# A spectral filter and a two-layer block on one core: the first batch's order of work, and the last chunk's stores

## The chip, the cores and the metric

The kernel runs on one core of a Trainium2 chip. The core has TensorE (PE, matrix products; its weight loads are shown apart as PEld), VectorE (DVE), ScalarE (ACT), GpSimd (POOL) and SyncE (SP, which only issues transfers). Transfers are issued from the queues of SP, ACT or POOL and carried out by 16 DMA engines. The metric is the device time of one execution in microseconds (us): the median of three runs before is 748.88 (748.31 to 749.69).

## The reference

```python
x: (8, 3008, 256)   filt_r, filt_i: (1505, 256)   w_in: (256, 2048)   w_out: (2048, 256)     # float32
X = np.fft.rfft(x, axis=1)
y = np.fft.irfft(X * (filt_r + 1j * filt_i)[None], n=3008, axis=1)    # a filter along the sequence
t = y.reshape(24064, 256)
h = t @ w_in
out = np.maximum(0.01 * h, h) @ w_out
```

## The kernel before

**The filter as matrix products.** 3008 = 94 x 32. A batch is transformed in four stages: s1 (94-point transform, one matmul for two of the 32 rows n2), s2 (twiddles and the 32-point transform, one matrix for each of 24 frequencies), the product with the filter, sa (inverse 32 points) and sb (inverse 94 points, which writes `yt`, the transposed activations of the current batch, 256 x 3008 in two halves dt). Between s1 and s2, and between sa and sb, the data must be turned. Batches 1 to 7 are turned through DRAM: staged in `st1` or `st2`, stored by SP to `dz1` or `dz2` (L264, L334), loaded back by SP (`t1_load` L271, `t2_load` L278). Every load of a batch's z1 needs all eight stores of its s1.

**The two-layer block.** Tokens go in 47 chunks of 512. `moe1` (L514) makes one column block ct of 16 for a chunk with two matmuls of 512; for every second ct ScalarE's leaky ReLU (L519) takes the pair from one of two wide accumulators (`ph`) to `gt`. The second layer of the first three chunks is `plain` (L639); from then on it is seven products of Strassen's scheme with 16 matmuls each (`products`, `product`, L578), whose sums VectorE makes (L551) and whose results VectorE combines into output rows (`rows`), stored by SP (`store`, L565).

**The loop's order** is a list sorted by plan time. SL = 8 units stand for one chunk; `PLANS` gives start and step of each stage of each batch in units, and a loop over a heap places the groups at least GAP = 0.6 units apart; z1 loads follow the last s1 group by AFTER[0] + LANDED = 2.96 units, and s2 a load by READ = 2.2. Each engine works through its own instructions in that order and waits on semaphores; POOL and SP, which have few, run ahead of TensorE.

**The first batch** has no earlier chunk to hide behind. Its steps are the string `FIRST`, executed one by one ahead of the loop: `xc` rounds early rows of x from fp32; `s1p` and `s1e` are s1's matmuls and their spread into big[0]; `t1` and `t2` are VectorE's transposes (big[0] to big[1], big[2] to big[0], four quarters each: quarters 0 and 1 are one half of the channels); `s2p` is s2's matmuls; the filter product is made by VectorE (`s2d`) or by ScalarE's copy (`s2a`, into one of six spare tiles) and POOL's product (`s2m`); `sap`, `sae` are sa and its copy, `sbp`, `sbe` sb and its copy to `yt`; `warm` is idle matmuls. A step's arguments are half, first row or frequency, count, part, accumulator (b0 to b4) or engine (A: ScalarE, D: VectorE). An `sb` group of half dt needs `t2` quarters 2 dt and 2 dt + 1.

Ahead of that string x comes in as follows: rows 0 to 5 by SP in fp32, rows 6 to 31 by three POOL transfers that round to fp16. POOL then issues the constants f2, the filter by halves of the channels, i1 and w_in, and, inside `FIRST`, the next batch's x in two halves and w_out. Ten of the sixteen last-stage groups are in `FIRST`; the other six are `late_sb`, put into the loop at the times `REST`. All of batch 1's s1 is in the loop.

**At the end** the last chunk has no later one beside it: its products run in the order m1, m7, m2, m6, m4, m5, m3, in turn on two accumulator banks, and its rows leave in 128 KB pieces. A tile of 128 tokens is one piece, or two where it crosses a boundary of 376 tokens.

Of the kernel before, what the change touches and what calls it, by code (L numbers as in the profile page):

```python
# [11 lines left out]
P = 128  # L12
# [63 lines left out]
def kernel(  # L76
# [134 lines left out]
    EARLY = 6  # L211
    x_early = big[1][:].bitcast(FP32)[:, : EARLY * D].rearrange("p (n d) -> p n d", n=EARLY)
    nc.sync.dma_start(small_sb[:], small_d.ap())
    nc.sync.dma_start(x_early[:R1], bass.AP(tensor=x.tensor, offset=x.offset, ap=[[N2 * D, R1], [D, EARLY], [1, D]]))
    for n0, nn in ((6, 10), (16, 10), (26, 6)):
        x_load(0, n0, nn)
# [8 lines left out]
    nc.gpsimd.dma_start(i1_sb[:], i1_d.ap())  # L225
    nc.gpsimd.dma_start(w_in_sb[:], moe_w_in.rearrange("(dt p) c -> p dt c", p=P))
# [27 lines left out]
    def s1_group(b, g, copy):  # L254
        def go():
            ps = bank("pf", 2, D)
            h = g // 2
            need(("x", b, h if b > 1 else 0), *[("st1", b, h - 4)] * (h > 3 and b > 1))
            nc.tensor.matmul(ps, fwd1[:N1], x_sb[:N1, ds(2 * g, 2), :], start=True, stop=True)  # L259
            issued.add(("s1", b, g))  # L260
            st = st1[h % 4] if b > 1 or h < 4 else st1_more[h % 4]
            copy(st[:, ds(2 * (g % 2), 2), :], ps)  # L262
            if g % 2:
                soon(AFTER[0], lambda: noted(("st1", b, h), lambda: nc.sync.dma_start(  # L264
                    dz1[b % 2][ds(4 * h, 4)].rearrange("n p d -> p n d"), st)))
        return go

# [95 lines left out]
    first_banks = single + wide  # L363
# [3 lines left out]
    def fill(key, b, n, w):  # L367
        held[key] = ps = first_banks[int(b[1:])][:, : n * w].rearrange("p (n w) -> p n w", n=n)
        return ps

    def keep_warm(n):
        for _ in range(n):
            nc.tensor.matmul(po_ps.rearrange("p a d -> p (a d)"), idle[:, 0:P], idle[:],  # L373
                             start=True, stop=True)

    def s1p(_, n0, n, b):
        ps = fill(("s1", n0), b, n, D)
        for j in range(0, n, 2):
            nc.tensor.matmul(ps[:, ds(j, 2), :], fwd1[:N1], x_sb[:N1, ds(n0 + j, 2), :],
                             start=True, stop=True)  # L380

    def s1e(_, n0, n, e):
        spread(big[0], n0, held.pop(("s1", n0)), engine[e])
# [6 lines left out]
    def s2p(hf, c, n, i, b):  # L390

        ps = fill(("s2", hf, c, i), b, n, DH)
        src = big[1][:].rearrange("p (n e r t) -> p n r e t", n=Q // 2, r=2, t=2)
        for j in range(n):
            v = src[:, (c + j) // 2, (c + j) % 2, ts(hf, DH // 2)]
            if i == 0:
                nc.tensor.matmul(ps[:, j, :].rearrange("p (e t) -> p e t", t=2), f2_sb[:, c + j, :], v,
                                 start=True, stop=True)
                continue
            for h in range(2):  # L400
                nc.tensor.matmul(ps[ts(h, 64), j, :].rearrange("p (e t) -> p e t", t=2),
                                 f2_sb[:, c + j, ts(1 - h, 64)], v, start=True, stop=True)
# [4 lines left out]
    def s2d(hf, c, n, i):  # L407
        times_filter(nc.vector, hf, c, n, i, held.pop(("s2", hf, c, i)))

    def s2a(hf, c, n, i):  # L410

        at_c = c if ("s2", hf, c, i) in held else c - 4
        held["xf", hf, c, i] = xf = spare.pop(0)
        key = ("s2", hf, at_c, i)
        act(xf[:], (held.pop(key) if c - at_c == n - 4 else held[key])[:, ds(c - at_c, 4), :])
# [35 lines left out]
    def late_sb(dt, h, copy):  # L451
        ps = bank("pf", 4, N1)
        sb_matmuls(ps, dt, h)
        quad_copy(h, dt, ps, copy)

    def load_x(half):
        x_load(1, half * N2 // 2, N2 // 2)
        issued.add(("x", 1, 0))

    def load_w_out():  # L460
        nc.gpsimd.dma_start(w_out_sb[:], moe_w_out.rearrange("(ct p) d -> p ct d", p=P))

    def round_x(n0, n, e):
# [3 lines left out]
        xc 0 4 A, xc 4 2 D, warm 18, s1p 0 0 4 b3, s1p 0 4 2 b0, warm 3, s1p 0 14 2 b1, s1e 0 4 2 D,  # L467
        s1e 0 0 4 A, s1p 0 10 4 b4, s1e 0 10 4 A, s1p 0 6 4 b3, s1e 0 14 2 D, warm 4, s1p 0 20 4 b4,
        s1e 0 6 4 D, s1p 0 16 4 b3, s1e 0 16 4 A, s1p 0 26 2 b2, s1p 0 24 2 b0, s1e 0 24 2 A, s1e 0 20 4 D,
        s1p 0 28 2 b1, s1p 0 30 2 b4, s1e 0 26 2 D, s1e 0 30 2 A, s1e 0 28 2 D, t1 0, t1 1, warm 14,  # L470
        s2p 0 0 4 0 b3, s2p 0 0 4 1 b2, warm 2, s2p 0 8 4 1 b0, s2a 0 0 4 0, s2a 0 0 4 1, t1 3,
        s2p 0 12 4 1 b4, t1 2, s2d 0 8 4 1, s2p 0 12 4 0 b1, s2p 0 16 8 0 b3, s2m 0 0 4 0, s2m 0 0 4 1,
        s2d 0 16 8 0, s2a 0 12 4 1, s2p 0 8 4 0 b2, s2p 1 16 8 0 b4, s2p 0 4 4 1 b0, s2a 0 12 4 0, s2d 0 8 4 0,
        s2a 1 16 8 0, s2p 0 4 4 0 b1, s2p 1 16 8 1 b3, s2d 0 4 4 0, s2a 1 20 8 0, sap 0 8 b2, s2d 0 4 4 1,
        s2a 1 16 8 1, s2a 1 20 8 1, s2m 0 12 4 0, s2p 0 16 8 1 b4, sap 0 0 b1, s2p 1 0 8 1 b3, s2m 0 12 4 1,
        sap 0 12 b0, s2m 1 20 8 0, sae 0 8 A, s2d 0 16 8 1, sae 0 0 A, s2p 1 8 8 1 b4, sap 0 4 b2, s2d 1 0 8 1,
        sap 0 16 b1, sae 0 12 A, s2p 1 8 8 0 b3, sap 0 20 b0, s2d 1 8 8 1, s2m 1 20 8 1, sae 0 4 A,
        s2d 1 8 8 0, s2p 1 0 8 0 b4, sae 0 16 A, sap 1 20 b2, s2d 1 0 8 0, sap 1 12 b1, sae 0 20 A, sap 1 8 b0,
        x 0, s2m 1 16 8 0, sae 1 20 A, s2m 1 16 8 1, x 1, w_out, sae 1 12 A, sae 1 8 A, sap 1 16 b3,
        sae 1 16 A, sap 1 4 b2, t2 1, sae 1 4 A, sap 1 0 b4, t2 0, sae 1 0 A, warm 4, sbp 0 1 b1, sbp 0 4 b0,  # L480
        sbp 0 0 b3, sbp 0 3 b2, t2 3, sbe 0 1 A, sbe 0 4 A, sbe 0 0 A, sbp 0 2 b4, sbp 0 7 b1, sbp 0 6 b0,
        t2 2, sbe 0 2 A, sbe 0 7 A, sbp 0 5 b3, sbp 1 0 b4, sbp 1 1 b1, sbe 0 6 A, sbe 0 5 A, sbe 1 1 A,
        sbe 0 3 D, sbe 1 0 D
    """
    steps = dict(s1p=s1p, s1e=s1e, t1=t1, s2p=s2p, s2d=s2d, s2a=s2a, s2m=s2m, sap=sap, sae=sae, t2=t2,
                 sbp=sbp, sbe=sbe, x=load_x, w_out=load_w_out, xc=round_x, warm=keep_warm)
# [15 lines left out]
    gts, osts, phs = {}, {}, {}  # L502
# [39 lines left out]

    def quarter(ci, i, j):
        return gts[ci][:, ts(j, NCH), ts(i, TH)]
# [12 lines left out]
    def store(ci, tj, of, queue=nc.sync):  # L557

        t, end = ci * CH + tj * P, ci * CH + (tj + 1) * P
        lo = 0  # L560
        while t < end:
            e = min(end, (t // QT + 1) * QT)
            b, h = divmod(t // QT, N2 // 4)
            row = b * N + (t % QT) // 4 * N2 + 4 * h
            queue.dma_start(  # L565
                bass.AP(tensor=out.tensor, offset=out.offset + row * D,
                        ap=[[N2 * D, (e - t) // 4], [D, 4], [1, D]]), of[lo : lo + e - t])
            lo, t = lo + e - t, e

    def product(ci, a, w, after, last_sum=None):  # L570

        po = out_banks[done["products"] % 2][:, 0]
        done["products"] += 1

        def one(t, c):
            if last_sum is not None:
                need(("sum", ci, last_sum))
            nc.tensor.matmul(po[:, t], a()[:, c, ts(t, P)], w[:, c, :],  # L578
                             start=(c == 0), stop=(c == NCH - 1))
            if t == 1 and c == NCH - 1:  # L580
                after(po)
        return [lambda t=t, c=c: one(t, c) for t in range(2) for c in range(NCH)]
# [7 lines left out]
    def stores(ci, i, of=range(2)):  # L590
        for j in of:
            store(ci, 2 * i + j, rows(ci, i)[:, j, 0:2, :].rearrange("p k d -> p (k d)"),
                  nc.scalar if ci == NCHUNK - 1 and i == j else nc.sync)
# [13 lines left out]
    def products(ci):  # L607
# [9 lines left out]
        def m2():  # L617
            return product(ci, a12, b21, lambda po: add(rows(ci, 0)[:, :, 0], po, t1, AL.add))
# [3 lines left out]

        if ci == NCHUNK - 1:
            items = last_product(ci - 1) + m1() + m7() + m2()
        elif ci > W0:
# [4 lines left out]
        items += product(ci, lambda: sum_places(ci)[2], wt[1], lambda po: add(part[1], twice(po), part[0], AL.add), 2)  # L630
        items += product(ci, a22, wt[3], lambda po: add(rows(ci, 1)[:, :, 0], po, u3, AL.add))
        items += product(ci, lambda: sum_places(ci)[0], wt[0], after5, 0)
        return items + last_product(ci) if ci == NCHUNK - 1 else items
# [15 lines left out]
    for g in range(10, 16):  # L649
        at(REST[g - 10], lambda g=g: late_sb(1, g - 8, (act, dve)[g % 2]))  # L650

    def plan(b, s1, s1_step, s2, s2_step, lag, sb, sb_step, xl, x_step):
        for g in range(16):
            groups.append((s1 + s1_step * g, 1, b, g, s1_group(b, g, dve if b == 1 and g % 4 < 3 else act)))
            if g % 2 and b + 1 < B:
# [28 lines left out]
    last, when, place, loads = -1, {}, {}, {}  # L684
# [32 lines left out]
    for ci in range(NCHUNK + 1):  # L717
        if ci < NCHUNK:
            for ct in range(NCT):
# [43 lines left out]
```

## Time and profile before

| | us |
|---|---|
| median of three runs | 748.88 |
| the profiled execution, time | 748.2 |
| its span, first to last instruction | 746.4 |
| first matmul of the loop (L514) | 34.56 |
| first s2 matmul of batch 1 (L308) | 59.64 |
| last matmul's end, by the chain of waits | 741.38 |

| engine | busy, us | share of the span |
|---|---|---|
| TensorE matmuls | 737.3 | 99% |
| weight loads | 528.6 | 71% |
| ScalarE | 559.1 | 75% |
| VectorE | 502.2 | 67% |
| GpSimd | 168.4 | 23% |

Matmuls are pipelined, so the duration of one (0.38 us for 512 columns) is longer than the distance to the next. The chain of waits goes back from the last instruction, at each step to what released it; its steps show what one instruction costs in a row of its kind. In the views of the queues q0 is POOL's queue and q1 SP's; a share over 100% is time of several packets at once on an engine.

### The profile page before, as it was taken

Reading aid. Unit: us, or ns where it says so; the run is one execution under the profiler, and the core shown is the slowest. Engines: PE = TensorE matmul, PEld = TensorE weight load, DVE = VectorE, ACT = ScalarE, POOL = GpSimd, SP = SyncE. Lnnn points to the kernel's source line nnn. Section 1 sums busy time; section 2 is a strip of 40 time slices with the busy share of each in tenths; the row PEclk is TensorE's granted clock in tenths of the full one; section 3 lists DMA queues with packets and bytes.
Section 4 is the critical chain, followed back from the end, with each engine's and each line's share of the span. In section 5 each row is a group of like instructions: output and inputs, shape, how many; then the busy total and the mean of one; then the engine's idle time right before and its main releaser. Section 6 shows DMA issues by size and latency. Waiting matters only on the chain.

```text
span 746.4 us, 19411 instructions
## 1 busy us (share of the span) xinstructions
PE 737.3 (99%) x8017; PEld 528.6 (71%) x8017; DVE 502.2 (67%) x684; ACT 559.1 (75%) x755; POOL 168.4 (23%) x171
## 2 busy tenths in 40 slices
PE   8999999999999999999999999999999999999997
PEld 3556667676687777877778777777777777777776
DVE  5987637776686766766767667766676676465565
ACT  4776797888878787877777777787777777777662
POOL 5603412332222222121332322121212210000000
PEclk9999999999999999999999999999999999999999
DMA  9997797978875666755675656544454333111012
GB/s 205 228 225 197 189 229 214 216 187 214 215 178 147 161 196 161 173 138 156 199 179 144 158 164 171 158 133 111 144 165 118 100 108 107 52 54 54 29 49 66
DMA packets 119560, 113.64 MB, mean 152 GB/s; under 512 B 16352, under 2 KB 92768, under 8 KB 119280
## 3 DMA queue, kind: packets, MB, share of 16 engines
q1 hardware_dynamic: 104128, 94.66, 42.6%
q0 software_dynamic: 15056, 17.49, 16.0%
q8 instruction: 62, 1.02, 0.6%
q10 hardware_dynamic: 288, 0.26, 0.1%
q14 instruction: 26, 0.21, 0.1%
HBM read 57.51 MB, written 50.33 MB: 144 GB/s over the span
## 4 chain that ended last, share of the span: by engine, by line
PE 95%; DVE 2%; DMA 1%; ACT 1%; issue 0%; SPq 0%; DVEq 0%; ACTq 0%
PE ph L514 43%; PE po_ps L578 18%; PE pf L578 18%; PE pf L259 3%; PE pf L351 3%; PE pf L308 2%; PE pf L330 2%; PE pf L639 1%; PE po_ps L639 1%; DMA big<-in_x_dram 1%; PE po_ps L373 1%; DMA dz<-big 0%; DVE big L551 0%; ACT yt L341 0%; PE pf L442 0%
## 5 line engine op out<-in xcount | busy, mean ns | idle before, releaser
L519 ACT ACTIVATE gt_c<-ph 128x1024 f16<-128x1024 f32 x376 | 385.3, 1025 | 133.5 <-PE ph L514 122.7
L514 PE MATMUL ph<-yt,w_in_sb 128*128 128x512 f16 (+7 forms) x1728 | 447.3, 351 | 0.2 <-ACT yt L341 0.2
L578 PEld LDWEIGHTS <-gt_c 128*128 128x128 f16 x2800 | 202.2, 98 | 91.1
L323 POOL TENSOR_TENSOR y_b_g<-p_b_g,p_b_g 128x512 f16<-128x512 f32 x84 | 118.7, 1414 | 413.1 <-DMA p_b_g<-p_b_g 222.9
L578 PEld LDWEIGHTS <-big 128*128 128x128 f16 x2128 | 151.3, 98 | 61.6 <-issue 0.2
L514 PEld LDWEIGHTS <-w_in_sb 128*128 128x128 f16 x1728 | 137.5, 98 | 19.7 <-DVE yt L341 0.4
L317 DVE TENSOR_TENSOR p_b_g<-pf,fb_sb 128x512 f32<-128x512 f32 x78 | 53.6, 688 | 31.6 <-PE pf L308 13.3
L578 PE MATMUL po_ps<-wt_sb,gt_c 128*128 128x128 f16 x704 | 70.0, 219 | 0.1
L578 PE MATMUL pf<-wt_sb,gt_c 128*128 128x128 f16 x688 | 68.4, 219 | 0.0
L578 PE MATMUL pf<-w_out_sb,gt_c 128*128 128x128 f16 x720 | 67.9, 219 | 0.0
L578 PE MATMUL po_ps<-wt_sb,big 128*128 128x128 f16 x720 | 67.4, 219 | 0.0
L578 PE MATMUL pf<-wt_sb,big 128*128 128x128 f16 x704 | 67.2, 219 | 0.0
L262 ACT CAST big<-pf 128x512 f16<-128x512 f32 x98 | 57.1, 588 | 11.9 <-PE pf L259 10.5
L578 PE MATMUL po_ps<-w_out_sb,gt_c 128*128 128x128 f16 x688 | 66.0, 219 | 0.0
L341 ACT CAST yt<-pf 128x376 f16<-128x376 f32 x120 | 56.3, 473 | 11.0 <-PE pf L351 8.1
L551 DVE TENSOR_TENSOR gt_c<-gt_c 128x2048 f16<-128x2048 f16 x43 | 57.2, 1331 | 1.0
L320 DVE TENSOR_TENSOR p_b_g<-pf,fa_sb 128x512 f32<-128x512 f32 x84 | 57.2, 680 | 0.2
L551 DVE TENSOR_TENSOR big<-gt_c 128x2048 f16<-128x2048 f16 (+1 forms) x46 | 55.8, 1214 | 0.1
L551 DVE TENSOR_TENSOR big<-gt_c,big 128x2048 f16<-128x2048 f16 (+1 forms) x45 | 55.8, 1240 | 0.0
L551 DVE TENSOR_TENSOR big<-big,gt_c 128x2048 f16<-128x2048 f16 (+1 forms) x45 | 55.4, 1232 | 0.1
L332 ACT CAST big<-pf 128x512 f16<-128x512 f32 x84 | 49.0, 584 | 4.9 <-PE pf L330 3.0
L259 PE MATMUL pf<-x_sb,small_sb 94*128 94x512 f16 x109 | 41.6, 381 | 0.0
(91 smaller groups left out, 621.9 us busy)
## 6 DMA issues: line engine op xcount, KB each, us to landing
dz<-big SPq DMA_DIRECT2D x98, 256.0 KB
p_b_g<-p_b_g SPq DMA_DIRECT2D x156, 128.0 KB
out_dram<-ost_c_h SPq DMA_DIRECT2D x118, 128.0 KB
big<-dz SPq DMA_DIRECT2D x42, 256.0 KB
big<-dz SPq DMA_DIRECT2D x56, 192.0 KB
x_sb<-in_x_dram POOLq DMA_DIRECT2D x40, 192.0 KB, 4.4
x_sb<-in_x_dram POOLq DMA_DIRECT2D x2, 768.0 KB, 9.3
w_in_sb<-in_moe_w_in_dram POOLq DMA_DIRECT2D x1, 1024.0 KB, 13.8
```

What stands on the lines that cost most here:

```text
L259: nc.tensor.matmul(ps, fwd1[:N1], x_sb[:N1, ds(2 * g, 2), :], start=True, stop=True)
L262: copy(st[:, ds(2 * (g % 2), 2), :], ps)
L317: nc.vector.tensor_tensor(p2[:], ps, fb, AL.mult)
L320: nc.vector.tensor_tensor(p1[:], ps, fa, AL.mult)
L323: ("y", b, g), lambda: nc.gpsimd.tensor_tensor(y1[:], p1[:], p3[:], AL.add)))
L332: nc.scalar.copy(st2[h % 4][:, ds(2 * (g % 2), 2), :], ps)
L341: copy(yv, ps.rearrange("p c a -> p a c"))
L351: nc.tensor.matmul(ps[:, j, :], z2[h % 4][:K4, j, ts(dt, P)], i1_sb[:K4, 4 * h + j, :], start=True, stop=True)
L514: nc.tensor.matmul(ph[:, j, ds(t - ci * CH, e - t)], w_in_sb[:, dt, ts(ct, P)], yt[:, dt, ds(t % N, e - t)], start=(dt == 0), stop=(dt == ...
L519: nc.scalar.activation(gts[ci][:, ds(2 * g, 2), :], ph, AF.Lrelu)
L551: nc.vector.tensor_tensor(*(v[:, ds(c0, n)] for v in (o, i0, i1)), op)
L578: nc.tensor.matmul(po[:, t], a()[:, c, ts(t, P)], w[:, c, :], start=(c == 0), stop=(c == NCH - 1))
```

## The change

- **x of batch 0.** Rows 0 to 11 come early in fp32, by two SP transfers of six rows; the rest by POOL in pieces of 8, 8 and 4. The small constants move from SP's queue to ScalarE's. Six `xc` steps of two rows round the early rows.
- **s1 by halves of the channels.** `s1p` and `s1e` take "a" (all 256), "l" or "r" (128 each). Rows 20 to 31 go by halves.
- **A sixth accumulator** for `FIRST`: the output bank po_ps is b3, the wide ones become b4 and b5. `warm` names its bank.
- **Moved into `FIRST`:** the six late last-stage groups; eight s1 groups of batch 1 (`bp`, `be`, with their stores to dz1 placed in the loop); the first four column blocks of chunk 0 (`la` and `lb` are the two halves of the contraction, `le` the leaky ReLU).
- **POOL's loads** become steps: x0 and i1 after the first transposes, then w_in in two halves (w0, w1), x1 and w_out after POOL's ten products.
- **A new order** of all steps.
- **The last chunk:** order m1, m7, m2, m6, m5, m4, m3, each from m6 on in banks of its own; the two halves of its tokens change places (`token_half`); the left half of the rows that m2 completes is stored at once; m4 and m3 are combined and stored tile by tile, by SP and ScalarE, the last ones as half rows (64 KB).
- **The planner** starts from the columns and groups already done (`begun`, `ahead`).

```diff
-    EARLY = 6
+    EARLY = 12
...
-    nc.sync.dma_start(small_sb[:], small_d.ap())
-    nc.sync.dma_start(x_early[:R1], bass.AP(tensor=x.tensor, offset=x.offset, ap=[[N2 * D, R1], [D, EARLY], [1, D]]))
-    for n0, nn in ((6, 10), (16, 10), (26, 6)):
+    for n0 in range(0, EARLY, 6):
+        nc.sync.dma_start(x_early[:R1, ds(n0, 6)], bass.AP(tensor=x.tensor, offset=x.offset + n0 * D,
+                                                           ap=[[N2 * D, R1], [D, 6], [1, D]]))
+    nc.scalar.dma_start(small_sb[:], small_d.ap())
+    for n0, nn in ((12, 8), (20, 8), (28, 4)):
         x_load(0, n0, nn)
...
-    nc.gpsimd.dma_start(i1_sb[:], i1_d.ap())
-    nc.gpsimd.dma_start(w_in_sb[:], moe_w_in.rearrange("(dt p) c -> p dt c", p=P))
...
-    first_banks = single + wide
+    first_banks = single + [po_ps.rearrange("p a d -> p (a d)")] + wide
...
+    halves = {"a": ds(0, D), "l": ds(0, DH), "r": ds(DH, DH)}
+    def s1p(d, n0, n, b):
+        at, w = halves[d], halves[d].size
+        ps = fill(("s1", d, n0), b, n, w)
+        m = CH // w
+        for j in range(0, n, m):
+            nc.tensor.matmul(ps[:, ds(j, m), :], fwd1[:N1], x_sb[:N1, ds(n0 + j, m), at], start=True, stop=True)
...
+    def load(what):
+        if what == "i1":
+            nc.gpsimd.dma_start(i1_sb[:], i1_d.ap())
+        elif what == "w_out":
+            nc.gpsimd.dma_start(w_out_sb[:], moe_w_out.rearrange("(ct p) d -> p ct d", p=P))
+        elif what[0] == "x":
+            x_load(1, int(what[1]) * N2 // 2, N2 // 2)
+            issued.add(("x", 1, 0))
+        else:
+            part = ts(int(what[1]), DFF // 2)
+            nc.gpsimd.dma_start(w_in_sb[:, :, part], moe_w_in.rearrange("(dt p) c -> p dt c", p=P)[:, :, part])
+    def next_s1p(g, b):
+        ps = fill(("next", g), b, 2, D)
+        nc.tensor.matmul(ps, fwd1[:N1], x_sb[:N1, ds(2 * g, 2), :], start=True, stop=True)
+    def next_s1e(g, e):
+        engine[e](st1_of(1, g // 2)[:, ds(2 * (g % 2), 2), :], held.pop(("next", g)))
+    def first_l1(k, dt):
...
+        if dt == 0:
+            first_ph[k] = bank("ph", 2, CH)
+        for j in range(2):
+            nc.tensor.matmul(first_ph[k][:, j, :], w_in_sb[:, dt, ts(2 * k + j, P)], yt[:, dt, :CH],
+                             start=(dt == 0), stop=(dt == NDT - 1))
+    def lrelu(k):
+        nc.scalar.activation(gts[0][:, ds(2 * k, 2), :], first_ph.pop(k), AF.Lrelu)
...
     FIRST = """
+        warm 13 b4, xc 0 2 A, xc 4 2 D, xc 2 2 D, s1p a 0 2 b0, warm 3 b2, xc 6 2 D, xc 8 2 A, s1e a 0 2 A,
...
+        s1p r 28 4 b0, s1p r 24 4 b2, s1e l 28 4 A, warm 13 b3, s1e a 10 2 D, s1e r 28 4 A, t1 0, s1e r 24 4 A,
+        t1 1, load x0, t1 3, s2p 0 4 4 0 b0, load i1, s2p 0 0 4 0 b1, s2p 0 12 4 1 b2, s2p 0 4 4 1 b3, t1 2,
...
+        sae 0 16 A, s2m 1 4 4 1, s2d 1 0 4 1, sap 1 16 b5, sae 1 8 A, s2p 1 20 4 1 b2, t2 1, sae 1 16 A, bp 4 b0,
+        s2m 1 12 4 1, bp 2 b1, be 4 A, bp 0 b3, sap 1 0 b5, s2d 1 20 4 1, be 2 A, bp 5 b0, s2m 1 12 4 0,
+        sap 1 4 b4, be 0 A, sae 1 0 D, sap 1 20 b1, be 5 A, t2 0, bp 7 b2, load w0, bp 1 b3, sae 1 4 A,
+        sap 1 12 b0, load w1, sae 1 20 A, sae 1 12 D, sbp 0 1 b5, be 1 A, load x1, sbp 0 0 b1, t2 2, sbe 0 1 A,
+        sbp 0 7 b4, load w_out, sbp 0 5 b3, sbe 0 0 A, sbp 0 6 b5, sbe 0 5 A, sbp 0 4 b1, t2 3, sbe 0 7 A,
...
+        be 7 D, sbp 1 0 b3, sbe 1 2 A, sbp 1 4 b1, la 0, sbe 1 0 D, sbe 1 7 A, sbe 1 4 A, bp 6 b0, la 1, be 6 A,
+        lb 0, lb 1, le 1, le 0
     """
...
+    def token_half(ci, i):
+        return 1 - i if ci == NCHUNK - 1 else i
...
+        if ci == NCHUNK - 1:
+            free = [w[:, :CH].rearrange("p (a t d) -> p a t d", a=2, t=2)[:, 0] for w in wide + single]
+            return last_product(ci - 1) + m1() + m7() + m2(ci) + m6(free[0]) + last_three(ci, free[1:])
...
+        def m4_tile(t, po):
+            add(high[:, t, 0], po, u3[:, t], AL.add)
+            parts = list(pieces(ci, t, high[:, t, 0:2, :].rearrange("p k d -> p (k d)")))
+            parts.sort(key=lambda v: -v[1].shape[0])
+            soon(0.02, lambda: (nc.sync, nc.scalar)[t].dma_start(*parts[0]))
+            for v in parts[1:]:
+                soon(0.6, lambda v=v: nc.sync.dma_start(*v))
+        def m3_tile(t, po):
+            add(low[:, t, 1], po, high[:, t, 2], AL.add)
+            soon(0.02, lambda: store(ci, 2 + t, low[:, t, 1], P, P, queue=(nc.sync, nc.scalar)[t]))
...
-    for g in range(10, 16):
-        at(REST[g - 10], lambda g=g: late_sb(1, g - 8, (act, dve)[g % 2]))
+    ahead, begun = FIRST.count(" bp "), 2 * FIRST.count(" lb ")
+    for h in range(ahead // 2):
+        at(begun / 2 + 0.7 + 0.8 * h, lambda h=h: st1_store(1, h))
...
-    last, when, place, loads = -1, {}, {}, {}
+    last, when, place, loads = begun / 2 - GAP, {(1, 1, g): 0 for g in range(ahead)}, {}, {}
...
-            for ct in range(NCT):
+            for ct in range(0 if ci else begun, NCT):
```

## The prediction, on record before any run of the change

> **What bounds the kernel now.** I read the page first: busy shares and slices, then the chain of waits.
>
> ```profile
> span 746.4 us, 19411 instructions
> ...
> PE 737.3 (99%) x8017; PEld 528.6 (71%) x8017; DVE 502.2 (67%) x684; ACT 559.1 (75%) x755; POOL 168.4 (23%) x171
> ...
> PE 95%; DVE 2%; DMA 1%; ACT 1%; issue 0%; SPq 0%; DVEq 0%; ACTq 0%
> ```
>
> The reader is to see that TensorE is the bound. From the first L514 matmul (34.56) to the last one (741.38) are 706.8 us. The steps of the chain price the work: 0.43 us for two 512-column matmuls (0.217 each), 0.44 for four of L639 (0.11), 0.39 for seven of L578 (0.056). Counted out over 47 chunks and seven batches this gives about 706, so the loop has no holes. Its time falls only by work that leaves TensorE's list, and any new wait in it is paid in full. Outside it lie 34.56 us ahead and 5.0 behind. The profiled execution took 748.2 us; the median of the runs is 748.88, 0.7 above it. Differences are added to 748.88.
>
> The chain of waits over the first 50 us:
>
> ```profile
> 27.75 1.21 DVE prod L405
> 28.96 2.29 DVE big L434 x2
> 31.30 0.46 PE pf L442 x8
> 31.78 2.74 ACT yt L341 x7
> 34.56 0.38 PE ph L514
> ```
>
> VectorE's filter products and transposes come last, then ScalarE's copies of the last stage. The timeline adds who feeds them:
>
> ```profile
> 16.80 0.71 POOL L226 DMA_DIRECT2D w_in_sb<-in_moe_w_in_dram  x1 [0.54 <-DMA fa_sb<-in_filt_i_dram]
> 18.23 4.52 POOL L405 TENSOR_TENSOR prod<-spare,fa_sb 128x512 f16<-128x512 f32 x4 [0.71 <-ACT spare L415]
> 23.05 2.29 POOL L405 TENSOR_TENSOR prod<-spare,fa_sb 128x512 f16<-128x512 f32 x2 [0.30 <-ACT spare L415]
> ...
> 28.12 0.57 POOL L196 DMA_DIRECT2D x_sb<-in_x_dram  x1
> 28.69 1.18 POOL L461 DMA_DIRECT2D w_out_sb<-in_moe_w_out_dram  x1
> ```
>
> At 23.05 POOL waits on "spare", but that copy ended by 21.6: the filter's second half landed then. w_in, second x and w_out were issued between POOL's products, so the DMA engines never ran dry: they are busy in every slice from 2 to 50 us. Two views of the queues over one microsecond each show who had them (packets, MB, share of the engines), the first from 39 to 40 us, the second from 42 to 43:
>
> ```profile
> q0 software_dynamic: 391, 0.20, 146.6%
> ```
> ```profile
> q1 hardware_dynamic: 442, 0.22, 78.1%
> ```
>
> Until w_out is through (about 41.6) POOL's queue has all of it; SP's first dz store, issued at 37.44, moves nothing before 41. Then SP's 2.9 MB (eight stores and the new f2) flow until 50 to 53, and the loads that need them follow:
>
> ```profile
> 37.44 1.55 SPq L264 DMA_DIRECT2D dz<-big  x2
> ...
> 40.41 10.68 SPq L264 DMA_DIRECT2D dz<-big  x6
> 51.18 4.26 SPq L565 DMA_DIRECT2D out_dram<-ost_c_t  x2
> 55.66 1.86 SPq L271 DMA_DIRECT2D big<-dz  x4
> ```
>
> **Moved work.** Out of the loop go eight s1 groups (8 x 0.217 = 1.73), four columns ct of chunk 0 (eight matmuls, 1.73) and six late sb (0.38 each, 2.28): 5.74 us. Break-even is therefore a loop that starts at 34.56 + 5.74 = 40.30.
>
> **New prologue.** The small constants (0.37 us of issue, 0.13 MB) leave SP's queue for ScalarE's, so the first six rows land some 0.8 us sooner (before: 6.88); rows 6 to 11 share with POOL's casts and land between 7.5 and 9.5. As fp32 they take 0.59 MB at 0.36 MB/us instead of 0.295 MB at 0.21: 0.2 us more, which the earlier start pays. The last rows stay at 12.3, where POOL's L204 saw them; their matmul (0.38) and spread (0.61) end at 13.3, and half-d lets the first two transposes start then, since they need the left half alone. VectorE's own list before them (six x casts and spreads, if rows 6 to 11 are late) makes it 14.2 at worst; before, 14.66. Four transposes at 1.16, then seven products of the first half at 0.62 (1.87 for three), end near 22.9; the filter's second half still lands at 23.2. So VectorE gains nothing: from 23.3 six products (3.7; fourteen in all where there were sixteen, POOL has ten for eight), t2 1.18, a product 0.62, two sae at 0.66, three more t2 (3.5) end at 33.8 against 33.59. ScalarE then carries more: copies of 512 come 0.48 apart (two in 1.07), sbe 0.36 apart (two in 0.85). From sae 1 16 (27.65) eight such copies 3.9, thirteen sbe 4.7, be 3 and be 6 1.0: 37.2; lb 1 is ready at 37.9; two Lrelu 2.0. They come as "le 1, le 0", while the loop's first matmul writes the bank of le 0, so TensorE waits for both: start 39.9 to 40.7. I take 40.3, the two last steps being the nearest rows: **0 us**, between -1.3 (transposes' gain passed on whole) and +1.5 (three missed copies).
>
> **Early clock.** The first idle matmuls are 0.43 apart, after 4.47 us 0.20. The new order leaves TensorE idle some 2 us near 8. The Trainium skill ("TensorE: Matmul & The Clock Gate", Part 1: The HAM clock gate) says an idle window of about 3.4 us halves the clock again. By it sixteen s1 matmuls could cost 3.5 us more; by the row, which holds a pause of 1.2 us without loss, nothing.
>
> **Loads.** x0 and i1 follow the filters (end 21.5): 0.79 MB at the 0.21 MB/us of casts, 0.77 MB at 0.36, done at 27.4. But w0, w1, x1 and w_out stand behind ten POOL products: from 17.9, ten at 1.13 end at 29.2. With an issue of 0.7 and 1 us to start, the engines idle about 3.5 us. The four need 2.5 + 2.5 + 3.75 + 5.4: w0 lands about 35 (la 0 needs 36.5, hidden), x1 about 41 (s1 g8 needs 41.6, no room), w_out's bytes end at 45, not 41.6, landing 46 to 48 where L639 wants it at 47.2. What is late next is batch 1's z1. POOL, which runs ahead, also puts four x loads of batch 2 behind w_out by 37 us; before, two. Two more are 0.39 MB, 1.9 us; dz had the larger share after 42 (78% against 38% for POOL's queue), so half of it counts. SP, which also runs ahead, issues the stores of the groups moved in and the new f2 from 32 us, behind w0 or among the four; the sum of the bytes stays. The backlog ends at 50 + 3.5 + 0.95 + 0.2 (more fp32 in x) = 54.65. Add 1.6 to land (last output bytes at 744.8, end 746.4) and 3.2 for z1, which is the median of a 128 KB x load: 59.45. Meanwhile the planner, with s1 finished at 7.36 units and not 9.68, puts the first s2 of batch 1 at 12.95 units, not 14.9: 40.3 + 12 columns 5.2 + eight s1 1.73 = 47.2, plus 4.95/8 of a chunk (32 x 0.217 + 64 x 0.11 = 14.0) and one s1: 56.1. TensorE would stand 3.35 us in all, at x1, w_out or this s2, with all chunk 1 behind it; on SP the output stores wait behind z1's loads. Bounds: 0 if dz writes pass everything (the last one issued at 48, 3.8 us as from 742.61 to 746.4, 3.2 for z1: 55.0, in time), 5.3 with a gap of 3.8, both x loads ahead, and z1 taking the 3.9 of 55.66 to 59.53 (61.4). I take **+3.35**, since the row at 39 us shows SP waiting behind POOL's loads, not passing them.
>
> The Trainium skill ("DMA: Bandwidth & Descriptors", Anatomy of one DMA) prices a POOL transfer at 2 us plus bytes over 436 GB/s. An estimate by that: the four loads (5.8 MB of source) end at 44.5, dz and f2 are out near 51, s2 is on time, and the sum is 747.6. The trace moved dz at 0.33 to 0.35 MB/us and landed w_out 15.9 us after its issue, where the page's price alone gives 6.8; so the measurement decides.
>
> **The end.**
>
> ```profile
> 741.23 1.47 ACTq L565 DMA_DIRECT2D out_dram<-ost_c_h  x2
> 741.40 0.42 DVE L603 TENSOR_TENSOR ost_c_h<-pf,ost_c_h 128x256 f32<-128x256 f32 x1 [0.20 <-PE pf L578]
> ...
> 742.61 0.91 SPq L565 DMA_DIRECT2D out_dram<-ost_c_h  x1
> ```
>
> Own banks remove the 0.2 us before 737.58 (m6 waited for L621). The last add shrinks from 0.42 to about 0.28 (512 columns 0.69, 256 0.42). One store of 64 KB on ACT replaces SP's two pieces: issue over at 742.2, not 743.5. The 512-byte runs may eat some. **-1.3**, between -1.7 and -0.5. Six adds by tile lie under the matmuls (0.45 a tile).
>
> **Sum.** 0 + 3.35 - 1.3 = +2.05: 750.9 us.
>
> **Rivals.** *The loads come in time.* For it: the before kernel had 1 us of slack at 55.66, and dz writes got the larger share after 42. Against: the idle gap. Stall 0 to 1: 748.88 - 1.3 + 0.5 = 748.1. *The prologue pays and loads come in time.* For it: transposes can start 1.25 sooner and ScalarE idles 1.9 us between 17 and 27.7. Against: the filter at 23.05. 748.88 - 1.3 - 1.3 = 746.3; it decides if the loop starts before 39.2 and s2 of batch 1 runs by 55. *The change does not do what it says*, the tail's small rows taking as long as before: 0.8 more on any of these.
>
> **Numbers.** Late loads 0.55 (749.4 to 752.9), in time 0.23, prologue pays 0.22. A measurement tells about 0.2% (1.5 us) from no change, so slower is 0.55, same 0.23 and faster 0.22. The range goes from 746.2, the paying prologue, to 752.9, the full price of late loads.
>
> **What would show it.** Right: TensorE idle for 2 us or more between 41 and 62 on x_sb, w_out_sb or big<-dz (L259, L639, L308); DMA near empty about 28 to 31; first loop matmul at 40.3 after le 0; last add to end 0.9 shorter. Wrong: no such wait, first s2 of batch 1 by 57; or a loop start before 39 or after 42.

## The result, and the profile after

The changed kernel takes **756.34 us** (754.87 to 762.95, 6 runs) beside 748.95 (748.07 to 749.69, 6 runs) of the kernel before on the same chip: ratio **1.0115 [1.0091, 1.0139]**. It is slower, as forecast, but by 7.4 us and not by 2; 756.3 lies above the range (746.2 to 752.9). The profiled execution took 755.19 us with a span of 753.4, 7.0 above the span before, and that difference is what follows.

The page of the changed kernel (busy shares and the share of each engine in the chain that ended last):

```profile
span 753.4 us, 19393 instructions
...
PE 737.0 (98%) x8001; PEld 528.5 (70%) x8001; DVE 499.4 (66%) x687; ACT 563.1 (75%) x767; POOL 168.4 (22%) x174
...
PE 90%; DMA 5%; POOL 2%; DVE 2%; issue 1%; ACT 0%; SPq 0%; POOLq 0%
```

TensorE's busy time is the same (737.0 after 737.3); most of the 7 us is time in which it stands. Transfers have gone from 1% of the chain to 5%. The whole list of what TensorE waited for after 40 us is below (line, releaser, us in all, times, longest); before, it held one entry of 0.2 us.

```profile
PE po_ps L722 <- DMA w_out_sb<-in_moe_w_out_dram: 3.1, 1, 3.1
PE ph L555 <- ACT gt_c L495: 2.1, 1, 2.1
PE pf L358 <- DMA big<-dz: 0.8, 1, 0.8
PE pf L315 <- ACT big L262: 0.6, 2, 0.4
PE pf L259 <- DMA x_sb<-in_x_dram: 0.3, 1, 0.3
PE po_ps L630 <- DVE big L680: 0.3, 1, 0.3
PE pf L358 <- DVE p_b_g L327: 0.2, 1, 0.2
```

The chain of waits from 30 to 63 us (start, us, what), and POOL's timeline that leads into it:

```profile
30.64 1.44 POOL w_in_sb L472 x2
32.07 11.55 DMA x_sb<-in_x_dram
...
43.66 0.59 PE pf L259
...
52.17 0.96 SPq L272
...
53.23 6.41 DMA dz<-big
...
59.83 2.97 DMA big<-dz
...
62.84 0.38 PE pf L315 x2
```
```profile
19.40 11.23 POOL L418 TENSOR_TENSOR prod<-spare,fa_sb 128x512 f16<-128x512 f32 x10 [1.23 <-ACT spare L426]
30.59 1.49 POOL L472 DMA_DIRECT2D w_in_sb<-in_moe_w_in_dram  x2
32.07 0.56 POOL L196 DMA_DIRECT2D x_sb<-in_x_dram  x1
32.60 1.20 POOL L466 DMA_DIRECT2D w_out_sb<-in_moe_w_out_dram  x1
```

The reader is to see one sequence: ten products in a row on POOL, then the four loads that the loop's start needs, then TensorE waiting at x1 (43.66) and at w_out (54.13). Batch 1's first s2 starts at 62.84 (before 59.64), as soon as its z1 has landed. Ahead of the loads the DMA engines stand empty. Four windows of the changed kernel (stretch; busy time and count of PE, PEld, DVE, ACT, POOL; granted clock; DMA share; GB/s):

```profile
12.00:14.00 2.00, 2.00 (x6) 0.73 (x5) 1.24 (x3) 1.40 (x3) 1.59 (x3) 0.50 1.44 275
...
28.00:30.00 2.00, 2.00 (x17) 0.95 (x16) 2.00 (x3) 2.00 (x6) 2.00 (x3) 1.00 0.05 21
30.00:32.00 2.00, 1.84 (x11) 0.62 (x10) 2.00 (x4) 2.00 (x6) 2.00 (x3) 1.00 0.04 8
...
44.00:46.00 2.00, 2.00 (x6) 0.73 (x5) 1.06 (x2) 0.86 (x1) 0.00 (x0) 0.52 1.06 345
```

A share of 0.05 and 0.04 is an empty engine, from about 28.3 to 32.5. In the first and the last of these windows the granted clock is half, and six matmuls fill 2 us.

Where the 7 us lie, in the prediction's terms, is read from two matmuls, the loop's first and the second layer's first:

```profile
41.54 1.81 PE L555 MATMUL ph<-yt,w_in_sb 128*128 128x512 f16 x6 [2.09 <-ACT gt_c L495]
...
54.13 0.61 PE L722 MATMUL po_ps<-w_out_sb,gt_c 128*128 128x256 f16 x4 [3.07 <-DMA w_out_sb<-in_moe_w_out_dram]
```

The loop starts at 41.54, 1.24 after its break-even of 40.30. To 54.13 pass 12.59 us. They hold eight s1 groups and thirteen columns, 26 matmuls of L555 (in the kernel before 34, seventeen columns, stand ahead of the same point, one column more than the chunk has). That is 34 matmuls at 0.217, or 7.38 us, so 5.21 are lost: 3.07 at w_out, 0.31 at x1, and of the other 1.8 most to matmuls at a granted clock of 0.63 and 0.52 from 42 to 46 us, behind the pauses. Waits of 0.2 to 0.8 us between 66 and 179 us add some 1.9; not all of it can count, since the sum asks for 1.3. The end gives 0.73 back (last matmul's end to the last instruction 4.29, before 5.02).

### The profile page after: what moved, and what is told of

The parts are those of the page before. It is cut to its first block, busy times and chain, and to the rows that moved or that the text cites. A ratio compares the mean times of both kernels' runs of the same rounds, so it can differ in the third digit from the quotient of the medians.

```text
span 753.4 us, 19393 instructions
## 1 busy us (share of the span) xinstructions
PE 737.0 (98%) x8001; PEld 528.5 (70%) x8001; DVE 499.4 (66%) x687; ACT 563.1 (75%) x767; POOL 168.4 (22%) x174
## 3 DMA queue, kind: packets, MB, share of 16 engines
q0 software_dynamic: 15328, 17.19, 15.9%
## 4 chain that ended last, share of the span: by engine, by line
PE 90%; DMA 5%; POOL 2%; DVE 2%; issue 1%; ACT 0%; SPq 0%; POOLq 0%
PE ph L555 41%; PE po_ps L630 18%; PE pf L630 18%; DMA x_sb<-in_x_dram 3%; PE pf L358 3%; PE pf L259 3%; PE pf L315 2%; PE pf L337 2%; DMA dz<-big 2%; POOL prod L418 1%; PE pf L722 1%; PE po_ps L722 1%; DMA big<-dz 1%; DVE big L596 1%; PE po_ps L382 0%
## 5 line engine op out<-in xcount | busy, mean ns | idle before, releaser
L555 PE MATMUL ph<-yt,w_in_sb 128*128 128x512 f16 (+7 forms) x1720 | 445.8, 352 | 2.1 <-ACT gt_c L495 2.1
L630 PEld LDWEIGHTS <-gt_c 128*128 128x128 f16 x2800 | 202.2, 98 | 91.4 <-issue 0.2
L330 POOL TENSOR_TENSOR y_b_g<-p_b_g,p_b_g 128x512 f16<-128x512 f32 x84 | 116.0, 1382 | 427.9 <-DMA p_b_g<-p_b_g 242.6
L630 PEld LDWEIGHTS <-big 128*128 128x128 f16 x2128 | 151.2, 98 | 61.4
L555 PEld LDWEIGHTS <-w_in_sb 128*128 128x128 f16 x1720 | 136.8, 98 | 21.4 <-issue 4.3
L630 PE MATMUL po_ps<-wt_sb,gt_c 128*128 128x128 f16 x704 | 69.8, 219 | 0.3 <-DVE big L680 0.3
L630 PE MATMUL pf<-wt_sb,gt_c 128*128 128x128 f16 x688 | 68.4, 219 | 0.0
L630 PE MATMUL pf<-w_out_sb,gt_c 128*128 128x128 f16 x720 | 67.9, 219 | 0.0
L630 PE MATMUL pf<-wt_sb,big 128*128 128x128 f16 x704 | 67.0, 219 | 0.0
L630 PE MATMUL po_ps<-w_out_sb,gt_c 128*128 128x128 f16 x688 | 66.0, 219 | 0.0
L630 PE MATMUL po_ps<-wt_sb,big 128*128 128x128 f16 x688 | 65.3, 219 | 0.0
L596 DVE TENSOR_TENSOR big<-gt_c 128x2048 f16<-128x2048 f16 (+1 forms) x46 | 58.2, 1265 | 0.1
L596 DVE TENSOR_TENSOR gt_c<-gt_c 128x2048 f16<-128x2048 f16 x43 | 55.5, 1291 | 1.0
L596 DVE TENSOR_TENSOR big<-big,gt_c 128x2048 f16<-128x2048 f16 (+1 forms) x45 | 54.1, 1203 | 0.1
L339 ACT CAST big<-pf 128x512 f16<-128x512 f32 x84 | 48.9, 583 | 4.1 <-PE pf L337 2.4
L259 PE MATMUL pf<-x_sb,small_sb 94*128 94x512 f16 x102 | 39.3, 386 | 0.4 <-DMA x_sb<-in_x_dram 0.3
```

The lines of the kernel that those rows point to most:

```text
L330: ("y", b, g), lambda: nc.gpsimd.tensor_tensor(y1[:], p1[:], p3[:], AL.add)))
L339: nc.scalar.copy(st2[h % 4][:, ds(2 * (g % 2), 2), :], ps)
L555: nc.tensor.matmul(ph[:, j, ds(t - ci * CH, e - t)], w_in_sb[:, dt, ts(ct, P)], yt[:, dt, ds(t % N, e - t)], start=(dt == 0), stop=(dt == ...
L596: nc.vector.tensor_tensor(*(v[:, ds(c0, n)] for v in (o, i0, i1)), op)
L630: nc.tensor.matmul(of[t], a()[:, c, ts(t, P)], w[:, c, :], start=(c == 0), stop=(c == NCH - 1))
```

## The experiments

Each ratio is against runs of the kernel before on the same chip.

**Early loads.** The order of POOL's loads alone: w0 goes ahead of the products and w1 behind the fourth, x1 and w_out stay.

```diff
- load i1, s2p 0 0 4 0 b1 ... load w0, bp 1 b3 ... sap 1 12 b0, load w1, sae 1 20 A
+ load i1, load w0, s2p 0 0 4 0 b1 ... s2m 0 16 4 0, load w1, ... bp 1 b3 ... sap 1 12 b0, sae 1 20 A
```

> The changed kernel, with w_in's two halves issued by POOL among its products (the first right after i1, the second after the fourth product) instead of behind all ten; x1 and w_out stay behind them. Theory (late loads: the DMA engines stand idle from 28.3 to 32.5 us and everything after is late): the idle stretch is filled, w_out lands by 50 us instead of 54.1, TensorE's wait for it falls from 3.1 us to under 1, x1 is there in time; time 750 to 752.5 us. Rival A (SP's dz stores and the new f2, which alternate with w_out packet by packet, make it late wherever it starts): w_out still lands after 52, time over 754. Rival B (the longer prologue itself is the loss): no more than 1.5 us gained.

Measured: 752.29 us, ratio 1.0061 [1.0046, 1.0076]. Its two windows from 28 to 32 us, and the only late load in its loop ahead of 62 us:

```profile
28.00:30.00 2.00, 2.00 (x16) 0.90 (x16) 2.00 (x5) 1.57 (x3) 2.00 (x3) 1.00 1.08 246
30.00:32.00 2.00, 2.00 (x17) 0.95 (x16) 2.00 (x4) 2.00 (x5) 2.00 (x3) 1.00 1.12 210
```
```profile
59.98 0.38 PE L315 MATMUL pf<-big,f_sb 128*128 128x256 f16 x2 [0.46 <-DMA big<-dz]
```

The engines stay full (1.08 and 1.12 where there was 0.05 and 0.04), the waits at x1 and w_out are gone, and 4.0 us come back by the medians (3.2 when each is taken against its own runs of the kernel before), although the loop starts later in this run (43.45, behind a granted clock of 0.50 from 12 to 18 us). Late loads are shown to be about half of the loss.

**Late loads in the kernel before.** The other way round: there, x0 goes early and w_in, x1 and w_out behind all POOL products.

```diff
-    nc.gpsimd.dma_start(w_in_sb[:], moe_w_in.rearrange("(dt p) c -> p dt c", p=P))
...
- t1 0, t1 1, warm 14, ... x 0, s2m 1 16 8 0, sae 1 20 A, s2m 1 16 8 1, x 1, w_out,
+ t1 0, t1 1, x 0, warm 14, ... s2m 1 16 8 0, sae 1 20 A, s2m 1 16 8 1, w_in, x 1, w_out,
```

> The kernel before with the loads alone moved: batch 1's x, first half, right after i1, and w_in, x's second half and w_out behind all of POOL's products; every other step in its old place. Theory (late loads): the DMA engines run dry for 2 to 4 us before 30, w_in or w_out are waited for, 753 to 756 us. Rival B (the longer prologue is the loss): under 751 us.

Measured: 750.24 us, 1.0038 [1.0024, 1.0052].

```profile
PE ph L516 <- DMA w_in_sb<-in_moe_w_in_dram: 1.7, 1, 1.7
...
PE po_ps L641 <- DMA w_out_sb<-in_moe_w_out_dram: 0.2, 1, 0.2
```

Late loads cost time here too, but 2.2 us. That is below the theory's 753 to 756, and where the rival, which blamed the longer prologue, had the time (under 751): w_in is waited for and w_out is nearly in time (18.6 us from issue to landing). The engines ran less dry, with shares of 0.32 and 0.82 from 26 to 30 us, and SP's stores come later here. So the order of the loads costs time by itself, but less than early loads give back in the changed kernel. What else that kernel loses is the subject of the runs further down.

**Who has the DMA engines.** The queues of the changed kernel from 44 to 46 us (packets, MB, share of the engines):

```profile
q1 hardware_dynamic: 140, 0.62, 80.2%
q0 software_dynamic: 141, 0.07, 26.0%
```

The two queues move packet for packet, 140 to 141, whatever a packet holds: q1's hold 4.4 KB on average (new f2; those of the dz stores hold 0.5), q0's 0.5 KB (w_out). In these 2 us w_out gets 0.07 MB; alone it gets 0.40 (below). From 39 to 40 us it is the other way round, with x1's packets of 8 KB beside the stores':

```profile
q0 software_dynamic: 23, 0.19, 89.7%
q1 hardware_dynamic: 23, 0.01, 5.8%
```

The Trainium skill ("DMA: Bandwidth & Descriptors", Queues, rings and completion order) has an engine go round the queues that have work and drain a whole packet, typically some 9 to 17 descriptors, from one before it switches. The equal counts agree with taking turns; how many descriptors one packet of these views stands for, none of them shows. To see whether that by itself costs time, SP's stores of the moved-in groups and the new f2 were planned later. By the plan times the stores follow those of groups 8 to 11, the first two that the loop itself makes, and the new f2 comes behind them (the expectation says rows 32 to 47; the rows of a batch run from 0 to 31, and groups 8 to 11 are rows 16 to 23):

```diff
-        at(begun / 2 + 0.7 + 0.8 * h, lambda h=h: st1_store(1, h))
+        at(begun / 2 + 4 + 0.1 * h, lambda h=h: st1_store(1, h))
...
-    F2T = 3.24
+    F2T = 6.5
```

> The changed kernel, but SP's transfers of the first eight moved-in groups (four dz stores) and the new f2 stand behind the stores of rows 32 to 47, so SP's queue moves nothing before about 44 us. Theory (the bytes of both queues set the end, and the alternation of their packets only says who waits): x1 lands at about 41 and w_out near 48 to 49 instead of 54.1, TensorE's waits for x1 and w_out go, but batch 1's z1 and first s2 come no earlier than in the changed kernel (62.8) or up to 2 us later, so the stall is there in place of them; 755.3 to 757. Rival (w_out's half share was itself the loss, z1 had room): 752 to 753.5, first s2 of batch 1 near 60.

Measured: 757.54 us, 1.0115 [1.0095, 1.0136]: the changed kernel's ratio, and 0.5 above the theory's range. The traced execution took 754.55, the shortest of the four. Its queues from 42 to 44 us, and the wait that replaced the one for w_out:

```profile
q0 software_dynamic: 774, 0.40, 145.0%
```
```profile
61.56 0.38 PE L315 MATMUL pf<-big,f_sb 128*128 128x256 f16 x2 [2.64 <-DMA big<-dz]
```

w_out lands 15.9 us after its issue (21.5 in the changed kernel) and nobody waits for it or x1, yet batch 1's first s2 comes only 1.3 us sooner than at 62.84 and now waits 2.64. The rival, which had z1 in time, falls: alternation decides which load is late, and taking it away gives no time back. That the bytes still to move at 32 us set the end agrees with this but isn't shown alone, since the chain to z1 also hangs on when the last store is issued, at 52.25 here and 53.23 in the changed kernel, each some 6 us from landing (5.94 and 6.41).

**A sooner start without sooner loads.** The changed kernel with `le 0, le 1` for `le 1, le 0`.

> The changed kernel with the two leaky ReLUs at the end of the first batch in the other order, le 0 before le 1, so that the accumulator that the loop's first matmul wants is free one activation (1.0 us) earlier. Theory (late loads): the loop starts at 40.5 instead of 41.5, but w_out lands at 54 as before, so the wait grows by what the start gains; time within 0.5 us of the changed kernel's. Rival B (prologue): 1.0 us less or more, since the clock may also stay up.

Measured: 756.43 us, 1.0128 [1.0100, 1.0156]. The loop starts at 39.68, 1.86 sooner, and all of it is given back. Not all of the 1.86 is the order of the two steps: in this trace the granted clock of the first stage was 1.00 and POOL's products began at 18.73, 0.67 sooner, with w_out 0.7 sooner too. The waits that take it back:

```profile
43.23 0.58 PE L259 MATMUL pf<-x_sb,small_sb 94*128 94x512 f16 x1 [2.04 <-DMA x_sb<-in_x_dram]
53.43 1.03 PE L722 MATMUL po_ps<-w_out_sb,gt_c 128*128 128x256 f16 x4 [2.27 <-DMA w_out_sb<-in_moe_w_out_dram]
```

**The halved clock of the first stage.** Eleven more idle matmuls in the changed kernel's two early pauses:

```diff
- warm 13 b4, xc 0 2 A, ... warm 3 b2, xc 6 2 D
+ warm 17 b4, xc 0 2 A, ... warm 10 b2, xc 6 2 D
```

> The changed kernel with eleven more idle matmuls in its two early pauses (17 for 13 ahead of the first x group, 10 for 3 ahead of the second), so that TensorE never stands idle for a microsecond before 10 us. Theory (the halved clock from 12 to 16 us put the first stage and so POOL's products late): granted clock 1.0 from 6 to 18 us, the first copy to spare at about 17.6 instead of 18.73, POOL's ten products done near 29.3 instead of 30.6, so w0, w1, x1 and w_out about 1.2 us earlier and the loop's first matmul near 40.3 instead of 41.54; 756.3 falls to 754.5 to 755.2. Rival (the first stage waits for x and for the filter's second half, not for the clock): clock 1.0 but POOL done after 30.2, 755.8 to 756.6.

Measured: 756.69 us, 1.0108 [1.0094, 1.0122]: no gain. The clock was as the theory had it, and the stage moved (first copy to spare 17.79 for 18.73, products from 18.46 to 29.8, loop start 40.93), but w_out landed when it had landed before:

```profile
12.00:14.00 2.00, 1.81 (x8) 0.67 (x7) 1.94 (x4) 2.00 (x5) 1.57 (x3) 1.00 1.38 280
```
```profile
54.10 1.03 PE L722 MATMUL po_ps<-w_out_sb,gt_c 128*128 128x256 f16 x4 [4.76 <-DMA w_out_sb<-in_moe_w_out_dram]
```

That the idle matmuls held the clock isn't shown by this run. The run with SP's transfers planned later has the changed kernel's list, and its two pauses were longer, 1.41 and 1.48 us, yet from 12 to 14 us it shows:

```profile
12.00:14.00 2.00, 1.99 (x10) 0.64 (x8) 1.86 (x3) 2.00 (x5) 1.52 (x3) 1.00 1.56 275
```

The run with the two Lrelu steps in the other order (pauses of 0.88 and 1.57) has 1.00 too; the one with early loads (1.38 and 1.52) has 0.50. So of four traces without the added idle matmuls two have the halved clock, and of the seven with them, this one and those below, none.

**Both edits.** Early loads and the idle matmuls together.

> Both edits: w0 and w1 issued among POOL's products and eleven more idle matmuls early. Theory: what was left of the loss with the early loads (752.3) is mostly the loop's late start of 43.45, and that comes from the halved clock of 12 to 18 us; start at 41.0 to 41.5, time 750.0 to 750.6. Rival (the extra issues on POOL put its products late, not the clock): start after 42.8, time 751.6 to 752.4.

Measured: 751.82 us, 1.0047 [1.0034, 1.0060]; loop start 41.86. The start meets neither side, the time is the rival's. Against the early loads alone (1.0061) the intervals overlap, so a gain of the clock in the time isn't shown.

**And le in the order of use.**

> Those two edits and the two last Lrelu steps in the order of use (le 0 ahead of le 1). Theory: with the loads in time, the loop can start about 1 us earlier and nothing behind it is late, so the gain isn't lost as it was with the order alone: 748.6 to 749.5, within 0.1% of the kernel before. Rival (transfers set the pace of the first 20 us of the loop anyway, the second first-stage store and batch 1's z1 last): same as without it, 750.0 to 750.6, with a longer wait at L315 or L358 on big<-dz.

Measured: 752.88 us, 1.0060 [1.0047, 1.0074]: no gain, and above both ranges. In this run POOL's products began at 20.58, in the one before at 19.48, though the lists are the same up to there: the filter landed later. Differences of 1 us between these versions can't be read from one profile.

**Less moved in.** First without `la`, `lb` and `le`; then also without `bp` and `be` of groups 4 to 7.

```diff
- la 0, sbe 1 0 D, sbe 1 7 A, sbe 1 4 A, bp 6 b0, la 1, be 6 A, lb 0, lb 1, le 1, le 0
+ sbe 1 0 D, sbe 1 7 A, sbe 1 4 A, bp 6 b0, be 6 A
```

> The kernel with early loads and idle matmuls, without the four moved-in columns of chunk 0 (la, lb and le leave the list, and the loop computes all sixteen). Theory (a moved step costs ScalarE more than TensorE gains, and ScalarE's list ends the prologue: the two Lrelu cost 2.56 us of start for 1.73 us of matmuls): the loop starts at 39.1 to 39.5 right behind the last s1 group, where its break-even is 38.57, and the time falls from 751.8 to 750.8 to 751.3. Rival (the four columns pay for themselves; the wait at le only stands in place of one for w0 or yt): start after 40.2, 751.8 or more.

> The same, and groups 4 to 7 of the next batch go back to the loop too (four s1 matmuls, 0.87 us of TensorE; four copies at 0.48 us, three of them ScalarE's). Theory (ScalarE's list): start 1.4 to 2 us earlier still, about 37.6, against a break-even of 37.70; 749.8 to 750.6, what is left being batch 1's z1 and first last-stage waits. Rival (the copies lie in holes of ScalarE): start within 0.6 us of the other kernel's and the time 0.3 us or more above it.

Measured: 752.48, 1.0047 [1.0033, 1.0060], and 750.48, 1.0023 [1.0014, 1.0032]. The first theory falls: the start was where it said (39.30), but what it brought went into waits behind it, 1.19 us for w_out, 1.52 for z1 and 1.8 at L358 (in the traced execution, the longest of five, 1.6 above their median). With four groups fewer the start is 37.48, just ahead of its break-even of 37.70 (38.57 less 0.87), no load is waited for ahead of 100 us, and 1.8 us come back (the intervals are apart), as its theory had it. What it still waits for in the loop:

```profile
PE pf L315 <- ACT big L339: 1.2, 3, 0.5
PE pf L358 <- DMA big<-dz: 0.9, 1, 0.9
PE pf L259 <- DVE p_b_g L327: 0.9, 1, 0.9
PE po_ps L629 <- DVE big L679: 0.2, 1, 0.2
```

These are 3.2 us; less 0.2 at the start and 0.7 at the end they give 2.3, which is its span (748.7) over that before (746.4).

**The planner's share.** On that version, the first last-stage groups of batch 1 later, and then its first s2 later too.

```diff
-            groups.append((min(sb + sb_step * g, due - DUE[0] + DUE[1] * (g % 2)), 4, b, g, sb_group(b, g, act)))
+            groups.append((min(sb + sb_step * g, due - (DUE[0] if b > 1 else 1.0) + DUE[1] * (g % 2)), 4, b, g, sb_group(b, g, act)))
...
-        (0.68, 0.31, 12.95, 0.9, 4.35, 38.33, 2.78, 7.78, 1.61),
+        (0.68, 0.31, 14.2, 0.9, 4.35, 38.33, 2.78, 7.78, 1.61),
```

> The smaller version (no moved-in last layer, four groups moved in, early loads, idle matmuls) with the first last-stage groups of batch 1 placed some 1.5 us later in the loop. Theory (what is left of its loss are a few waits of TensorE in the loop, each paid in full: 0.95 us at L358 for z2, 0.85 at L259, 1.2 at L315): the wait at L358 goes, nothing else moves, 749.4 to 749.9 against 750.5. Rival (such a wait only moves on to the next wait): 750.3 to 750.7.

> The same with batch 1's first s2 group planned at 14.2 units instead of 12.95 (the kernel before ran it at about 14.9). Theory: an s2 that comes as early as 12.95 is what crowds VectorE and ScalarE in the first chunks, so the waits at L259 and L315 shrink by about 1 us: 748.4 to 749.2, level with the kernel before (748.9) or a little under it. Rival (the three waits at L315 of 0.4 us come from the alternation of s1 and s2 and stay, and the last stage is late by what s2 is late): 749.6 to 751.

Measured: 751.51, 1.0046 [1.0032, 1.0060], and 749.83, 1.0023 [1.0014, 1.0032]. The first is a miss: L358 waits no more, but two matmuls then wait 0.50 and 0.69 us for yt, which the same groups make. With the later s2 the waits at L259 and L315 are gone as expected, the two for yt stay, others of 0.2 to 0.5 come at L337 and L358, and the time is in the rival's range, with the ratio of the version without either edit. No version with moved work beats the kernel before.

**The end alone.** The kernel before with only the last chunk's new order, banks and stores.

> The kernel before with the last chunk's new order, banks, token halves and stores alone. My forecast was -1.3 us; the trace of the changed kernel has 4.29 us from the last matmul to the end where it was 5.02, and no gap of 0.2 before m6 or another in its place, so -0.5 to -1.0: 748.0 to 748.5 us. Rival: nothing, 748.9.

Measured: 747.49 us (10 runs; before 748.08, 14 runs), ratio 0.9995 [0.9986, 1.0004]. The profiled span is 1.2 shorter (745.2), the medians 0.6; the interval doesn't tell it from none. The median of the spans is 0.95 shorter, but in all ten runs the time lies 2.14 to 2.23 us above the span, in the fourteen before 1.77 to 1.89; where these 0.35 us come from, no run shows.

## Why the prediction missed

**The bound: right.** TensorE's busy time didn't change, and its long waits in the loop were paid in full; of the small late ones (1.9 us) the sum has room for 1.3. The rival that had the loads in time and the one that had the prologue pay are out: the waits on x_sb and w_out_sb stand at the lines named (L259, and L722 which was L639), and the DMA engines were empty where the prediction put the gap.

**The start: inside its bounds, at the wrong end.** "I take 40.3", bounds -1.3 to +1.5; measured 41.54. POOL's products ran from 19.40 to 30.6, not from 17.9 to 29.2. In the three traces with the clock at full and the loads in this order they began at 18.46 to 18.73, so 0.7 to 0.9 of that goes with the clock and the rest with a first copy that came later than in the sum. The loop's first matmul waited for both Lrelu, as said (2.09 us).

**The clock: the row chosen gave no loss, and it was wrong.** The row had one pause of 1.2 us. The new order had two, of 1.13 and 1.26, with 1.0 us of matmuls between, and the granted clock was 0.95, 0.50 and 0.70 from 10 to 16 us. Pauses of that length don't decide it: two of four traces with these first steps kept 1.00, one of them with two longer pauses. The Trainium skill ("TensorE: Matmul & The Clock Gate", Part 1: The HAM clock gate) has the clock set by how busy the array has been over a free-running window; both outcomes from one list agree with that, but no view here shows where the windows lie. The price of 3.5 us isn't seen in the time: with the clock held in this stage, the time stayed (1.0108 and 1.0115), because the loads set the end. The sum had no clock for the loop itself, and there it does count: it is most of the 1.8 us lost besides waiting ahead of 54.13. The six runs of the changed kernel roughly follow their mean granted clock, from 0.997 at 754.87 us to 0.988 at 762.95 (0.998 to 1.000 in the fourteen of the kernel before beside the first experiments).

**The loads: the step that failed.** The mechanism was right, the term too small: +3.35 predicted, 5.21 measured ahead of 54.13, next to the upper bound of 5.3. "w_out's bytes end at 45, not 41.6, landing 46 to 48": it landed at 54.1, and x1 at 43.62 and not 41. The sum also had w_out wanted at 47.2; it counted twelve columns where thirteen run, so from the measured start it was wanted at 48.9. The gap was 4.2 us and not 3.5, a small part. The larger part is the reason given for the +3.35: "the row at 39 us shows SP waiting behind POOL's loads, not passing them". In the kernel before, SP's first store moved some 3.6 us after its issue at 37.44, as w_out's bytes ended, so that row fits a wait behind w_out and a slow start alike. In the changed kernel the first store, issued at 32.57, moved from 37 us on, 4.4 us after its issue, with nearly all of w_out still to come, and from then on the queues went packet for packet. The estimate gave the loads all of the engines first; with both queues at work x1, w_out and the stores all came late. The last store, which the prediction's lower bound had issued at 48 and 3.8 us from landing, was issued at 53.23 and took 6.41, and batch 1's first s2 came at 62.84 and not at 59.45.

**Behind it: not in the sum.** Some 1.3 us of later waits, at L358, L315 and L630, stood in the sum at nothing. The prediction ended its look at the first s2. In the version with half the groups and loads in time, such waits are all that is left of the loss.

**The end: right in sign, half in size.** -0.73 in the changed kernel's trace, -1.3 predicted, inside its bounds of -1.7 to -0.5. The last add ends 3.98 us before the last instruction (before 4.58), 0.6 less and not 0.9. The sum had the last store's issue over 0.8 us after the last matmul (742.2); it was over 1.92 after it, before 2.14, since it stood behind another store on ScalarE's queue:

```profile
748.56 1.75 ACTq L706 DMA_DIRECT2D out_dram<-ost_c_h  x1
750.40 0.63 ACTq L616 DMA_DIRECT2D out_dram<-ost_c_h  x1
```

The sum by its own terms: +1.24 and +5.21 and about +1.3 and -0.73 make 7.0, where the prediction had 0, +3.35, nothing and -1.3. Each stated term lies inside its own bounds. The range's upper end was too low because it takes the loads alone at their worst (748.88 + 5.3 - 1.3 = 752.9), with the start at 0 and the best guess for the end: here start, loads and end were all on their bad side, and the later waits came on top.

## What to carry to other kernels

A product moved onto an engine that also issues loads delays all loads behind it: look for the stretch in which the DMA engines run dry, and price what is still to move afterwards and the clock behind each pause, not only the wait that shows. When two queues have work, count on packets in turn, so that small packets lose to large ones; a queue that seems to wait for another may only be starting. Where several terms of a sum can go wrong together, let the range hold them together. Work moved ahead of a loop pays only if its start stays below the break-even and nothing that the loop takes early was paced by the old start; here a start 1.86 us sooner brought nothing.

## What the runs showed of the hardware

- Two queues with work took turns by packets of unlike size: 140 of 4.4 KB against 141 of 0.5 KB in 2 us, 0.62 MB against 0.07, and in the same kernel 23 of 0.5 KB against 23 of 8 KB in 1 us.
- A store's first packets moved about 4 us after its issue in three traces (37.44 to 41, 32.57 to 37, 34.24 to 38), and about 2 us after it in the run that held SP back (46.0 to 48). The other queue was full in all four, so what sets this time stays open.
- Two pauses of 0.9 to 1.6 us, 2.4 to 2.9 us in all within some 4 us, were followed by a granted clock of 0.50 in two traces and by 1.00 in two others with the same first steps. One of 1.2 us alone was followed by 1.00.
- The first stage's end moves by more than 1 us between runs of one list (products from 19.35 to 20.82 in six kernels with the same steps up to there, all at a granted clock of 1.00). What makes the filter land later stays open, and so does the split of the 1.7 us by which the best version, the last one with the later s2, misses the kernel before: its loop starts 0.45 after break-even in the trace, and it waits 2.3 us in the loop.
